# Sliding-window attention and a routed feed-forward, mixed by a gate: values projected transposed and turned on the core, and where the program jumps

## The chip, the core and the metric

The kernel runs on one core of a Trainium2 chip. The core has five engines with instruction streams of their own: TensorE (PE in the profile, its weight loads PEld), VectorE (DVE), ScalarE (ACT), GpSimd (POOL) and SyncE (SP), which here only issues DMA transfers. They meet through semaphores. SBUF is the on-chip memory, PSUM the eight banks that TensorE writes, HBM the memory outside the core. The metric is the time on the device in microseconds (us), the median of several runs.

## The reference

2048 tokens of 512 numbers in bf16. One branch is attention with 32 heads of 16 and a causal window of 256, the other a feed-forward that only the eight tokens with the largest router value pass. A sigmoid gate mixes them.

```python
def _A_ref(x, wqkv, wo):                       # S = 2048, D = 512
    H = 32; Dh = 16; W = 256
    q, k, v = split(x @ wqkv)                  # each by heads
    scores = einsum("bhqd,bhkd->bhqk", q, k) * Dh ** -0.5
    mask = (i - j >= 0) & (i - j < W)
    p = softmax(where(mask, scores, -1e9))
    return merge_heads(einsum("bhqk,bhkd->bhqd", p, v)) @ wo

def _B_ref(x, w_r, w_gate, w_up, w_down):      # w_gate, w_up: 512 x 1792
    r = x @ w_r
    idx = argsort(-r)[:, :8]                   # the top 8 tokens
    y = (silu(x[idx] @ w_gate) * (x[idx] @ w_up)) @ w_down
    return x.at[idx].add(y * sigmoid(r[idx]))

g = sigmoid((x * gate_w).sum(-1))              # x = A_x; _B_ref gets B_x in the call
out = g * _A_ref(x, wqkv, wo) + (1 - g) * _B_ref(x, ...)
```

The kernel reads A_x for both branches.

## The kernel before, in words

There are two programs in it. `fast_path` takes the softmax without subtracting a maximum; it adds up a flag that says whether all sums stayed in range. `general_path` is a slow one for other inputs; it does not run here. At the end every engine loads the flag and branches: to `fk_done`, or to `fk_general`.

**Chunks and units.** The 32 heads are done in 4 chunks c of 8 heads (128 columns). A chunk has 64 units, one for each block of 32 keys, so there are 256 units u. A unit (`s_unit`) is two score matmuls on TensorE (L690: the blocked keys Kbd against 288 queries QT, one for each half of the heads), one exponential on ScalarE (L697: 128 partitions x 576 columns from PSUM to P in SBUF) and, for each two units, one multiply by the mask on GpSimd (L704). P lies in a ring `PT` of RING slots, two slots a unit. `pv` (L725) multiplies P with the values: for each block of 128 queries, 34 columns of `Vbd` at a time (heads of 16 columns, and a column of ones that sums P); VectorE then takes the reciprocal of the sums (L740) and multiplies (L744), and a transposing DMA (`tr_dma`, L772) puts the result into OT, from which the output is projected (`wo_pair`, L788) and mixed (`out_evict`, L778).

**Projections.** x is brought in transposed, as XT, by transposing DMAs (L474) in pieces of 2, 2, 4, 4 and 4 tiles of 128 tokens. Q and K of a chunk are projected in squares of 512 tokens (`qk_pair`; 16 matmuls, L583); VectorE casts both to SBUF (L561, L564) and spreads K into Kbd with four masked multiplies (L569). The first square goes in two halves through `qk_first` (L604, L612, L615). Two PSUM bank pairs serve all work but the scores, and pass from one item to the next.

**Values.** `v_pair` (two chunks) and `v_two` (two chunks at once) project V with the tokens on the partitions (L626, L648). VectorE casts into `Vn` (L637, L660), and each piece is written to a scratch in HBM, `vsc` (L639, L663). `v_read` (L672) reads it back, for each group of 32 partitions, in another order of tokens, since `Vbd` needs each block of 32 keys on the 32 partitions of a head group, and zeros in the places of the other head. The zeros are written once at the start, by ScalarE (L530) and four DMAs (L534).

**Router.** `wrg_item` (L813) transposes the two weight rows of router and gate, `z_item` (L826) projects all tokens on them, `top_item` turns r into a row by way of a DMA (`f_r_row<-f_rT`) and searches the top 8 (L854, L855); ScalarE takes the sigmoid of these (L856). Then come a gather of eight rows, the feed-forward (`gu_item`, `silu_item`, `down_item`), a scatter into a copy of x, and `reload_x`, which loads that copy for the mix.

**What sets the order.** Operations are logged with a key (about the unit where they belong) and with costs and latencies; `schedule` walks through them, gives each engine what is ready with the smallest key, and so writes one fixed row of instructions for each engine, which then run in that order. A table `SHIFT` adds an offset to the keys of named groups. Each engine stops at an instruction whose semaphore isn't up yet.

**Blocks of code.** The engines' rows stand in one block; it ends with a barrier, then `values_load` and the branch:

```python
        bad = nc.values_load(flag[0:1, 0:1])                           # L1054
        ...
            br = eng.br_cond(bad < 1, "fk_done", "fk_general")         # L1058
            if et == mybir.EngineType.PE:
                br.branch_hint(S.hint["pe"])
            if et == mybir.EngineType.SP:
                br.branch_hint(S.hint["sp"])
        with nc.body("fk_general"):
            ...
            general_path(nc, *args)
            nc.br("fk_done")
        nc.switch_bb("fk_done")
```

The code of `general_path` lies between the branch and `fk_done`. A hint (a prefetch of the branch's target) stands 40 operations ahead of the end on TensorE and 8 on SyncE.

## Time and profile before

| | us |
|---|---|
| median of 3 runs | 203.36 (202.37 to 203.96) |
| the profiled execution | 203.8 |
| its span, first to last instruction | 202.1 |
| TensorE / ScalarE / VectorE / GpSimd busy | 168.3 / 147.3 / 110.7 / 87.6 |
| the 256 exponentials (L697) | 140.9 |
| casts of V (L637, L660) | 5.2 and 5.7 |

Times in the profile count from the first instruction. Busy time says how long an engine had something to do, not that it set the pace; the idle time before a group of instructions and what ended it (the arrow) say who waited for whom. "PEclk" is the clock granted to TensorE, 1.00 being full. An instruction is named by engine, line (L), operation and output<-input, with the number of instructions behind an x.

### The profile page before, as it was taken

What the parts mean: (1) busy time and instruction counts of PE and PEld (TensorE: products, weight loads), DVE (VectorE), ACT (ScalarE), POOL (GpSimd) and SP (SyncE); (2) the same over time, 40 slices, a digit from 0 to 9 for tenths busy, and PEclk for the clock granted to TensorE, in tenths of its full rate; (3) what the DMA queues carried; (4) which work ended last, traced back from release to release, by engine and by line L of the source; (5) the groups of instructions that cost most, each with busy time, mean ns of one, the idle gap of its engine ahead of it and who ended that gap; (6) DMA issues with size and microseconds to landing.
All of it is one profiled execution on the core that took longest, in us unless ns stands there. A gap on an engine that the chain in (4) does not pass through costs nothing.

```text
span 202.1 us, 10131 instructions
## 1 busy us (share of the span) xinstructions
PE 168.3 (83%) x4568; PEld 108.3 (54%) x4568; DVE 110.7 (55%) x287; ACT 147.3 (73%) x266; POOL 87.6 (43%) x142
## 2 busy tenths in 40 slices
PE   7639898899887699869977989999793889999970
PEld 2435656568465455636845536665562456476430
DVE  5503709837353935833625564499974354454780
ACT  6733860999992969657977897996897699999200
POOL 4112420555562355433543555663554345566200
PEclk9975759999996669856999999999999589999998
DMA  7997143168665733562175671378253102032221
GB/s 147 221 200 172 51 110 98 42 157 170 152 174 174 220 74 73 150 190 58 39 218 144 165 136 30 81 182 213 57 135 113 29 1 82 20 118 68 80 84 63
DMA packets 45217, 23.71 MB, mean 117 GB/s; under 512 B 32352, under 2 KB 44912, under 8 KB 45040
## 3 DMA queue, kind: packets, MB, share of 16 engines
q1 hardware_dynamic: 44048, 22.73, 45.4%
q8 instruction: 37, 0.61, 1.3%
q10 hardware_dynamic: 1056, 0.26, 0.6%
q14 instruction: 12, 0.10, 0.2%
q0 software_dynamic: 64, 0.02, 0.0%
HBM read 14.03 MB, written 6.43 MB: 101 GB/s over the span
## 4 chain that ended last, share of the span: by engine, by line
PE 42%; ACT 26%; DVE 13%; SPq 6%; DMA 5%; issue 5%; POOL 0%; DVEq 0%
ACT f_PT L697 26%; PE f_ps L583 12%; PE f_ps L690 11%; PE f_ps L725 8%; SPq L474 5%; PE f_ps L648 3%; PE f_ps L626 3%; PE f_ps L788 2%; DMA f_xw<-f_xc 2%; DVE f_Kr L564 2%; DVE f_QT L561 2%; DMA f_r_row<-f_rT 2%; DVE f_Kbd L569 2%; DVE f_xw L935 2%; PE f_ps L919 2%
## 5 line engine op out<-in xcount | busy, mean ns | idle before, releaser
L697 ACT ACTIVATE f_PT<-f_ps 128x576 bf16<-128x576 f32 (+7 forms) x256 | 140.9, 623 | 35.6 <-PE f_ps L690 23.4
L704 POOL TENSOR_TENSOR f_PT<-f_PT,f_MK 128x256 bf16<-128x256 bf16 (+1 forms) x128 | 83.4, 652 | 99.4 <-ACT f_PT L697 98.9
L690 PE MATMUL f_ps<-f_QT,f_Kbd 64*128 64x288 bf16 (+7 forms) x512 | 76.8, 300 | 9.7 <-ACT f_PT L697 7.5
L725 PE MATMUL f_ps<-f_Vbd,f_PT 64*128 64x34 bf16 x2880 | 56.7, 177 | 10.7 <-issue 5.0
L725 PEld LDWEIGHTS f_ps<-f_Vbd,f_PT 64*128 64x128 bf16 x2880 | 52.3, 95 | 22.6 <-issue 9.9
L690 PEld LDWEIGHTS f_ps<-f_QT,f_Kbd 64*128 64x128 bf16 x512 | 25.6, 97 | 35.3 <-ACT f_PT L697 28.9
L583 PE MATMUL f_ps<-f_XT,f_W 64*128 64x512 bf16 x240 | 43.8, 441 | 0.5 <-DVE f_On L744 0.5
L569 DVE TENSOR_SCALAR f_Kbd<-f_Kr,f_hm 128x512 bf16<-128x512 bf16 (+1 forms) x64 | 23.5, 426 | 0.1
L564 DVE CAST f_Kr<-f_ps 128x512 bf16<-128x512 f32 x15 | 10.2, 683 | 18.9 <-PE f_ps L583 18.8
L583 PEld LDWEIGHTS f_ps<-f_XT,f_W 64*128 64x128 bf16 x240 | 12.5, 107 | 8.8 <-issue 2.5
L561 DVE CAST f_QT<-f_ps 128x512 bf16<-128x512 f32 x15 | 10.2, 683 | 12.7 <-PE f_ps L583 12.7
L788 PE MATMUL f_ps<-f_wo,f_OT 64*128 64x512 bf16 x112 | 16.6, 377 | 0.1
L740 DVE RECIPROCAL f_RC<-f_ps 128x16 f32<-128x16 f32 (+1 forms) x33 | 8.2, 247 | 14.9 <-PE f_ps L725 13.7
L778 DVE SCALAR_TENSOR_TENSOR f_outt<-f_ps,f_g_f,f_xw 128x512 bf16<-128x512 f32 x16 | 11.4, 746 | 8.3 <-PE f_ps L788 8.2
L626 PE MATMUL f_ps<-f_W,f_XT 64*128 64x128 bf16 x256 | 13.9, 252 | 1.2 <-DMA f_XT<-in_A_x_dram 1.1
L744 DVE TENSOR_TENSOR f_On<-f_ps,f_RC 128x256 bf16<-128x256 f32 (+1 forms) x33 | 13.6, 412 | 0.7
L626 PEld LDWEIGHTS f_ps<-f_W,f_XT 64*128 64x128 bf16 x256 | 11.0, 112 | 3.5 <-issue 1.8
L648 PE MATMUL f_ps<-f_W,f_XT 64*128 64x256 bf16 x128 | 9.9, 270 | 0.2
L935 DVE TENSOR_SCALAR f_xw<-f_xw,f_omg_f 128x512 bf16<-128x512 bf16 x16 | 7.4, 500 | 2.8 <-DMA f_xw<-f_xc 2.8
L660 DVE CAST f_Vn<-f_ps 128x256 bf16<-128x256 f32 x16 | 5.7, 417 | 4.9 <-PE f_ps L648 4.9
L648 PEld LDWEIGHTS f_ps<-f_W,f_XT 64*128 64x128 bf16 x128 | 5.9, 94 | 1.8 <-PE f_ps L648 0.5
L637 DVE CAST f_Vn<-f_ps 128x512 bf16<-128x512 f32 x8 | 5.2, 672 | 2.8 <-PE f_ps L626 2.8
(91 smaller groups left out, 74.5 us busy)
## 6 DMA issues: line engine op xcount, KB each, us to landing
f_xc<-in_A_x_dram SPq DMA_DIRECT2D x8, 256.0 KB, 4.2
f_xw<-f_xc SPq DMA_DIRECT2D x8, 256.0 KB, 3.7
out_dram<-f_outt SPq DMA_DIRECT2D x16, 128.0 KB, 1.7
f_xw<-in_B_w_gate_dram SPq DMA_DIRECT2D x8, 224.0 KB, 3.2
f_xw<-in_B_w_up_dram SPq DMA_DIRECT2D x8, 224.0 KB, 3.5
f_xw<-in_B_w_down_dram SPq DMA_DIRECT2D x7, 256.0 KB, 4.1
f_vsc<-f_Vn SPq DMA_DIRECT2D x8, 136.0 KB, 3.2
f_Vbd<-f_vsc SPq DMA_DIRECT2D x16, 68.0 KB, 2.5
```

Of the source, the lines that this page charges most:

```text
L561: dve(lambda e: e.tensor_copy(out=dst, in_=bank(b)), r=[T(b)], w=[("QT", c % 2, tc)], cost=610, key=key, rel=rel)
L564: dve(lambda e: e.tensor_copy(out=Kr[:, tc, :], in_=bank(b)), r=[T(b)], w=[("Kr", tc)], cost=610, key=key, rel=rel)
L569: dve(lambda e, h=h, k0=k0, q=q: e.tensor_scalar(out=Kbd[:, c % 2, k0:k0 + w8, h, :], in0=Kr[:, tc, 32 * w8 * q:32 * w8 * q + 32 * w8].rea ...
L583: return e.matmul(bank((A, B)[which])[:, w0:w1], W[R, kc, f0:f0 + 128], XT[R, kc, 512 * tc + w0:512 * tc + w1], start=st, stop=False, skip ...
L626: return e.matmul(bank((A, B)[b])[:, 128 * i:128 * i + 128], XT[R, kc, 128 * a:128 * a + 128], W[R, kc, f0:f0 + 128], start=st, stop=False ...
L648: return e.matmul(bank((A, B)[b])[:, 256 * i:256 * i + 256], XT[R, kc, 128 * a:128 * a + 128], W[R, kc, f0:f0 + 256], start=st, stop=False ...
L690: ins = e.matmul(bank(b0 + s)[:, 0:n], Kbd[R, c % 2, kb, :, :].rearrange("p h k -> p (h k)"), QT[R, c % 2, 32 * kb:32 * kb + n], start=Tru ...
L697: act(lambda e: e.activation(out=dst, in_=ps[:, b0:b0 + 2, 0:n], func=ACT.Exp, scale=0.25), r=[T(b0), T(b0 + 1)], w=[("P", slot // 2), ("E ...
L704: pool(lambda e: e.tensor_tensor(out=v, in0=v, in1=m, op=ALU.mult), r=[("P", sl // 2), ("P", sl // 2 + 1)] + MKR, w=[("Pm", sl // 4)], cos ...
L725: ins = e.matmul(bank((A, B)[rg])[:, col:col + 34], PT[R, o0:o0 + 128], Vbd[R, c % 2, :, kb % 4, kb // 16, s, (kb // 4) % 4, :], start=(kb ...
L744: dve(lambda e: e.tensor_tensor(out=dst, in0=both(h_)[:, :, 0:68 * nj].rearrange("p b (j g d) -> p b j g d", d=17, g=4)[:, :, :, :, 0:16], ...
L788: return e.matmul(bank((A, B)[o])[:, w0:w1], OT[R, c, 128 * a:128 * a + 128], wo[R, c, w0:w1], start=st, stop=False, skip_group_check=True ...
```

## The change

1. **Values.** `v_order` (GpSimd) reorders the columns of W for V into `WV`. `v_pair`, now for all chunks, projects V transposed: WV is the stationary side and 512 tokens move, so that the features lie on the partitions. VectorE transposes each bank in squares of 32 into `TV` (f32), and two masked multiplies write it into `Vbd`, one for each of the two heads, which also writes the zeros. `Vn`, `vsc`, `v_two`, `v_read` and the zeros at the start are gone; the column of ones is written by two VectorE operations in `late_consts`, behind the first K.
2. **Jumps.** There is no barrier block. A few first operations of ACT, DVE, POOL and SP ("early": the first loads, the table, some constants) and all of TensorE's stand in the first block; each engine then jumps over the general code to `fk_main`. There the rest stands, each engine waits for the flag's semaphore, loads the flag and branches to `fk_done`, which now lies right behind. Hints: at the start on ACT and SP, 60 operations ahead of its jump on PE.
3. **Router** keys move by 2 to 4 units (22 to 26, 24 to 28, 40 to 42); RING goes from 40 to 48; costs and latencies in the list change, and 91 lines of `SHIFT` with them.

The core of the diff:

```diff
-RING = 40
+RING = 48
@@ emit
+            for i, op in enumerate(self.ops[e][:n]):
+                if e == "pe" and i == n - HINT_AT:
+                    hint = h.mark_branch_hint_location()
+                self.one(e, h, op)
+            br = h.br("fk_main")
+            if hint is not None:
+                br.branch_hint(hint)
...
+    def main(self):
+        for e in self.ENGS:
+            h = self.handle[e]
+            for op in self.ops[e][self.n_early[e]:]:
+                self.one(e, h, op)
+            h.wait_ge(*self.flag)
@@ fast_path
+        for op in S.log:
+            op.early = True
...
+        def late_consts():
+            dve(lambda e: e.memset(pads, 0.0), r=[("Krb", 0)], w=["pads"], cost=1900, key=K0 + 150)
+            for b in range(2):
+                dve(lambda e, b=b: e.tensor_scalar(out=Vbd[:].rearrange("p c s k b d -> p (c s k) b d")[:, :, b, 16], in0=bass.AP(ones_c, 0, [[128, 128], [0, 2], [1, 128]]),
+                                                   scalar1=pm[:, b:b + 1], scalar2=None, op0=ALU.mult), ...)
@@ v_pair
-                return e.matmul(bank((A, B)[b])[:, 128 * i:128 * i + 128], XT[R, kc, 128 * a:128 * a + 128], W[R, kc, f0:f0 + 128],
+                return e.matmul(bank((A, B)[b]), WV[R, c % 2, kc, :], XT[R, kc, t0:t0 + 512],
                                 start=st, stop=False, skip_group_check=True, tile_position=(R.start, 0))
...
-                dve(lambda e, b=b, g=g: e.tensor_copy(out=Vn[:, g, c % 2, :, :, :, 0:16], in_=bank((A, B)[b]).rearrange("p (i s h d) -> p h s i d", i=4, s=2, h=4)), ...)
-                dma(lambda e, g=g: e.dma_start(vsc[c].rearrange("h p g x -> p h g x")[:, :, g, :], Vn[:, g, c % 2].rearrange("p h s b d -> p h (s b d)")), ...)
+                dve(lambda e, b=b: e.transpose(out=TV[:, b, :], in_=bank((A, B)[b])), r=[T((A, B)[b])], w=[("TV", b)], cost=720, key=key, rel=h_)
+                for q in range(2):
+                    dst = Vbd[:, c % 2, :, 16 * tc:16 * tc + 16, q, 0:16].rearrange("p s k d -> p k s d")
+                    (dve if VM[q] == "dve" else pool)(
+                        lambda e, b=b, q=q, dst=dst: e.tensor_scalar(out=dst, in0=TV[:, b, :].rearrange("p (k s d) -> p k s d", s=2, d=16),
+                                                                     scalar1=pm[:, q:q + 1], scalar2=None, op0=ALU.mult), ...)
@@ router
-        at(21, lambda: wrg_item(22))
-        at(21.1, lambda: z_item(24))
-        at(36, lambda: top_item(40))
+        at(25, lambda: wrg_item(26))
+        at(25.1, lambda: z_item(28))
+        at(38, lambda: top_item(42))
@@ the r row's transfer, as the list counts it
-            dma(lambda e: e.dma_start(r_row[0:1, :], rT[:, :]), r=["rT"], w=["r_row"], key=key)
+            dma(lambda e: e.dma_start(r_row[0:1, :], rT[:, :]), r=["rT"], w=["r_row"], key=key, lat=4000)
@@ end
+        nc.switch_bb("fk_main", parent=first)
+        S.main()
+        bad = nc.values_load(flag[0:1, 0:1])
+        nc.br_cond(bad < 1, "fk_done", "fk_general")
+        nc.switch_bb("fk_done", parent=first)
```

What the list makes of it is seen in three places. First TensorE's row at the start, before: L604 is the first K and Q, L690 scores (four instructions are two units), L626 values, L813 the router's transpose. L583, K and Q of the next square, follows further down, and the first L725 stands behind 22 units.

```order
L604 MATMUL f_ps<-f_XT,f_W 128x256 x16
L690 MATMUL f_ps<-f_QT,f_Kbd 128x288 x4
L626 MATMUL f_ps<-f_W,f_XT 128x128 x8
L690 MATMUL f_ps<-f_QT,f_Kbd 128x288 x2
L626 MATMUL f_ps<-f_W,f_XT 128x128 x12
L690 MATMUL f_ps<-f_QT,f_Kbd 128x288 x2
L626 MATMUL f_ps<-f_W,f_XT 128x128 x12
L813 MATMUL f_ps<-f_ident,f_wrow 128x8
```

The row at the same place in the changed kernel, where L614 is the first K and Q, L679 scores, L593 K and Q of the next square and L644 values:

```order
L614 MATMUL f_ps<-f_XT,f_W 128x256 x16
L679 MATMUL f_ps<-f_QT,f_Kbd 128x288 x8
L593 MATMUL f_ps<-f_XT,f_W 128x512 x4
L679 MATMUL f_ps<-f_QT,f_Kbd 128x288 x2
L593 MATMUL f_ps<-f_XT,f_W 128x512 x4
L679 MATMUL f_ps<-f_QT,f_Kbd 128x288 x2
L644 MATMUL f_ps<-f_XT,f_WV 128x512 x2
L593 MATMUL f_ps<-f_XT,f_W 128x512 x2
```

Four units instead of two come first, and the second square of K and Q goes ahead of the values. The router's transpose (now L802) has moved from behind 4 units of scores to behind 20, its projection (now L815) from behind 8 to 15 units to behind 27 to 30, the first PV (now L714) to behind 14, and the transpose of r from behind 54 units to behind 49. In ScalarE's row the sigmoid of the top 8 moves from behind 68 exponentials to behind 71.

Second, VectorE's row between the first K and the second half of V. Before (L637 V, L561 and L564 casts of Q and K, L569 Kbd, L830 and L833 the router's z):

```order
L615 TENSOR_SCALAR f_Kbd<-f_Kr,f_hm 128x8x32 x4
L814 COPY f_wrg<-f_ps 128x8
L637 CAST f_Vn<-f_ps 128x32x16 x2
L561 CAST f_QT<-f_ps 128x512
L564 CAST f_Kr<-f_ps 128x512
L569 TENSOR_SCALAR f_Kbd<-f_Kr,f_hm 128x8x32 x8
L830 COPY f_zr<-f_ps 128x32
```

After (L544 and L546 the constants, L574 and L571 casts of K and Q, L579 Kbd, L655 the transpose and L659 the multiplies of V):

```order
L625 TENSOR_SCALAR f_Kbd<-f_Kr,f_hm 128x8x32 x4
L544 MEMSET f_PT 128x49x48
L546 TENSOR_SCALAR f_Vbd<-f_ones_c,f_pm 128x256 x2
L574 CAST f_Kr<-f_ps 128x512
L571 CAST f_QT<-f_ps 128x512
L579 TENSOR_SCALAR f_Kbd<-f_Kr,f_hm 128x8x32 x4
L655 STREAM_TRANSPOSE f_TV<-f_ps 128x512 x2
L659 TENSOR_SCALAR f_Vbd<-f_TV,f_pm 128x16x2x16 x4
L571 CAST f_QT<-f_ps 128x512
```

The memset of P's gaps has moved from the program's start to behind the first K, and two casts have become two transposes and four multiplies.

Third, the end on VectorE, before (the last mixes, the flag, the end of the block with its barrier, the load of the flag, the branch) and after:

```order
L778 SCALAR_TENSOR_TENSOR f_outt<-f_ps,f_g_f,f_xw 128x512 [waits fd_15]
L1041 TENSOR_SCALAR flag<-f_ps 1x1 [waits fk_pe]
L266 UNCONDITIONAL_BRANCH
L1054 TENSOR_LOAD flag [waits barrier_Pool_Activation_PE_DVE_SP_release]
L1058 COMPARE_AND_BRANCH
```

```order
L767 SCALAR_TENSOR_TENSOR f_outt<-f_ps,f_g_f,f_xw 128x512 [waits fd_9]
L767 SCALAR_TENSOR_TENSOR f_outt<-f_ps,f_g_f,f_xw 128x512 [waits fd_11,fk_pe]
L1019 TENSOR_SCALAR flag<-f_ps 1x1 [waits fk_pe]
L1038 TENSOR_LOAD flag [waits fk_dve]
L1039 COMPARE_AND_BRANCH
```

The flag is loaded behind its own semaphore instead of a barrier. TensorE's row ends, after the last matmul, with its jump to `fk_main`.

## The prediction

> **What bounds the kernel now.** I read the page first (busy line, clock row), then busy time by stage, then the waits of ScalarE (ACT), then the stretches with the longest waits in order of time.

> ```profile
> span 202.1 us, 10131 instructions
> PE 168.3 (83%) x4568; PEld 108.3 (54%) x4568; DVE 110.7 (55%) x287; ACT 147.3 (73%) x266; POOL 87.6 (43%) x142
> PEclk9975759999996669856999999999999589999998
> ```

> No engine is full on average. The clock row is the hint: slices (5 us each) with 5 or 6 come after stalls. So I cut the span where it changes.

> ```profile
> core 0: us, PE busy (x) PEld busy (x) DVE busy (x) ACT busy (x) POOL busy (x), PEclk, DMA share, GB/s
> 8.00:36.00 28.00, 22.04 (x489) 14.60 (x489) 11.35 (x38) 13.06 (x23) 6.77 (x10) 0.76 0.58 131
> 36.00:62.00 26.00, 23.04 (x780) 16.46 (x780) 13.89 (x32) 24.76 (x48) 14.77 (x23) 0.97 0.59 134
> 62.00:75.00 13.00, 10.03 (x181) 6.24 (x176) 7.86 (x17) 7.37 (x14) 5.09 (x7) 0.67 0.65 179
> 197.30:202.10 4.80, 0.00 (x0) 0.00 (x0) 0.00 (x0) 0.00 (x0) 0.00 (x0) 0.81 0.18 58
> ```

> In 36 to 62 ACT is full (24.8 of 26 us): there the exponentials set the pace. In 8 to 36 it works 13 of 28 us, in 62 to 75 7.4 of 13, and in the last 4.8 us nothing works. The losses lie in these places, and its waits say so:

> ```profile
> ACT f_PT L697 <- PE f_ps L690: 23.4, 33, 3.3
> ACT f_PT L697 <- PE f_ps L725: 10.7, 6, 5.2
> ACT f_sg L856 <- DVE f_top L854: 3.9, 1, 3.9
> ```

> The opening in order of time, exponentials first (count behind the x), then four of TensorE (PE): its last wait for x, the router's transpose, the first PV and a piece of K/Q at full clock:

> ```profile
> 8.03 1.19 ACT L697 ACTIVATE f_PT<-f_ps 128x576 bf16<-128x576 f32 x2 [0.39 <-PE f_ps L690]
> ...
> 14.30 0.65 ACT L697 ACTIVATE f_PT<-f_ps 128x576 bf16<-128x576 f32 x1 [3.18 <-PE f_ps L690]
> ...
> 21.06 4.84 ACT L697 ACTIVATE f_PT<-f_ps 128x576 bf16<-128x576 f32 x8 [3.26 <-PE f_ps L690]
> ...
> 35.36 1.19 ACT L697 ACTIVATE f_PT<-f_ps 128x576 bf16<-128x576 f32 x2 [5.19 <-PE f_ps L725]
> ```

> ```profile
> 9.37 0.40 PE L626 MATMUL f_ps<-f_W,f_XT 64*128 64x128 bf16 x8 [1.11 <-DMA f_XT<-in_A_x_dram]
> ...
> 13.74 0.16 PE L813 MATMUL f_ps<-f_ident,f_wrow 8*128 8x8 bf16 x1 [3.06 <-DMA f_wrow<-in_gate_w_dram]
> ...
> 32.00 1.63 PE L725 MATMUL f_ps<-f_Vbd,f_PT 64*128 64x34 bf16 x116 [0.65 <-DVE f_g_f L836]
> ...
> 34.19 1.04 PE L583 MATMUL f_ps<-f_XT,f_W 64*128 64x512 bf16 x8
> ```

> Three waits, 3.2 + 3.3 + 5.2 = 11.7 us. The first: PE stands 3.06 us at the router's tiny transpose (L813) until its weights land. The second follows at half clock. The third: the ring of P holds 20 units, 20 exponentials are done at 30.1, and the 21st waits until 35.36 for the first PV, which stands behind 22 units in PE's row and begins at 32.0.

> **The change part by part.** (1) Opening. The router's transpose now stands behind 20 units of scores instead of 4 and its projection behind 27 to 30, the first PV behind 14 instead of 22, the ring holds 24 units. Nothing in PE's row waits for those router weights any more. What is late next is the second K/Q square: its x is there at 9.4 (the L626 row, on the same tiles); its 16 matmuls take 2.1 us by the L583 row (eight in 1.04, a pair 0.26), and four score pairs between them 0.6 (288 of 512 columns, 0.15 each): 12.1; two casts of 0.68 (L564 below), so unit 8 has its Q at 13.5, against 8.03 + 8 x 0.605 (the row of eight: 4.84/8) = 12.9 at ACT's own pace. Unit 20 then is at 8.03 + 20 x 0.605 + 0.6 = 20.7; I take 22, one more for what I don't see. Gain to there 35.36 - 22 = **13.4**.

> Whether VectorE (DVE) lets that happen:

> ```profile
> L564 DVE CAST f_Kr<-f_ps 128x512 bf16<-128x512 f32 x15 | 10.2, 683 | 18.9 <-PE f_ps L583 18.8
> L637 DVE CAST f_Vn<-f_ps 128x512 bf16<-128x512 f32 x8 | 5.2, 672 | 2.8 <-PE f_ps L626 2.8
> L660 DVE CAST f_Vn<-f_ps 128x256 bf16<-128x256 f32 x16 | 5.7, 417 | 4.9 <-PE f_ps L648 4.9
> L523 DVE MEMSET f_PT<- 128x1968 uint32 x1 | 1.7, 1698 | 1.3 <-PEq L1937 1.3
> ```

> ```profile
> 7.94 0.87 DVE L615 TENSOR_SCALAR f_Kbd<-f_Kr,f_hm 128x256 bf16<-128x256 bf16 x4
> ...
> 34.12 1.13 DVE L569 TENSOR_SCALAR f_Kbd<-f_Kr,f_hm 128x512 bf16<-128x512 bf16 x4
> ...
> 37.83 1.96 DVE L569 TENSOR_SCALAR f_Kbd<-f_Kr,f_hm 128x512 bf16<-128x512 bf16 x4
> ```

> No row shows the transpose in squares of 32. It reads 512 f32 columns of PSUM as L637 does: 0.67 each, with 0.28 (an SBUF pass of 512) and 1.34 (twice the cast) as ends. The masking multiply reads 512 f32 from SBUF: between 0.28 (L569 at 34.12, 1.13 for four, GpSimd (POOL) idle) and 0.67; I take 0.45, near the 0.49 of the x4 at 37.83. A V pair is 2 x 0.67 + 4 x 0.45 = **3.2 us** (1.7 to 5.4), eight pairs 25 against the 10.9 of L637 and L660: 14 more (3 to 32). In the opening DVE's row is, from 8.8 (end of the first Kbd): memset 2.0 (1698 x 49/41 gaps of the ring), ones 0.6, two casts from 12.1 to 13.5, four half Kbd 0.9 (the L615 row), V pair 3.2: 17.6. PV behind 14 units is wanted at 8.03 + 14 x 0.605 + 0.6 = 17.1. So it fits, barely.

> ```profile
> 36.63 0.67 POOL L704 TENSOR_TENSOR f_PT<-f_PT,f_MK 128x256 bf16<-128x256 bf16 x1 [5.82 <-ACT f_PT L697]
> 37.77 0.67 POOL L704 TENSOR_TENSOR f_PT<-f_PT,f_MK 128x256 bf16<-128x256 bf16 x1 [0.47 <-ACT f_PT L697]
> ```

> POOL stood still for 5.8 us ahead of 36.6, so beside the first L569 row no mask ran, and beside the second one did: same shape, 0.28 against 0.49. [...]

> (2) Work put off. By unit 20 the kernel before had projected V of the second half and z; now they come between units 22 and 34, with the last K/Q square.

> ```profile
> L826 PE MATMUL f_ps<-f_wrg,f_XT 64*128 64x2 bf16 x128 | 2.8, 163 | 0.0
> ```

> Twelve units leave PE 12 x (0.605 - 0.15) = 5.5 us beside the scores. It needs V 2.1 and K/Q 2.1 (16 matmuls each, as above), z 2.8, PV 1.1 (80 by the 32.00 row): 8.1, so 2.6 over; DVE I put at 2 over, as V's 3.2 and the square's 3.1 (two casts, four Kbd of 0.44) meet there. I charge **+4.5** (1 to 8).

> (3) Router chain.

> ```profile
> 63.73 2.28 DVE L854 MAX8 f_top<-f_r_row 1x8 f32<-1x2048 bf16 x1 [4.76 <-DMA f_r_row<-f_rT]
> 66.05 0.21 ACT L856 ACTIVATE f_sg<-f_top 1x8 f32<-1x8 f32 x1 [3.92 <-DVE f_top L854]
> ```

> ACT stands 3.9 us at the sigmoid, behind 68 units. In its new row it stands behind 71, and the transpose of r goes from behind 54 to behind 49: 22 units instead of 14 between the two, some 5 us more. The wait should go (0 to -3.9): **-3**, and -1 for the half clock behind it (0.67 in 62 to 75). The two searches of 2.3 us stay on DVE.

> (4) The rest. Units 68 to 255 see five V pairs of 3.2 instead of 8 us of casts: 8 us more DVE work in a stretch where ACT is often the pace. No row excludes all or nothing: **+2** (-2 to +8). The 48 transfers of the V scratch and four of zeros leave the SP queue; ACT waits for none of them by the rows above, so 0.

> (5) The two ends.

> ```profile
> 195.44 0.39 PE L1038 MATMUL f_ps<-f_ones_f,f_okc 128*1 128x1 f32 x10
> 196.88 0.13 DVE L1041 TENSOR_SCALAR flag<-f_ps 1x1 int32<-1x1 f32 x1
> 196.33 0.99 SPq L780 DMA_DIRECT2D out_dram<-f_outt  x2
> L1058 SPq COMPARE_BRANCH  x1: 78/78/78, 198.3 to 198.3; - x1
> out_dram<-f_outt SPq DMA_DIRECT2D x16, 128.0 KB, 1.7
> ```

> The branch runs at 198.3, the span ends at 202.1: a jump taken costs 3.7 us, though SP has a prefetch hint ahead of it. After the change the last branch falls through, but the last output (issued 197.0, median 1.7 to land) holds the end to about 199.0, and PE has a jump of its own behind its last matmul: 195.8 + 3.7 + 0.6 for flag and branch = 200.1 if its hint fails. Gain 2.0 to 3.1: **-2.5**. The early jumps: DVE's memset is done at about 0.9, the jump makes it 4.6, 13 small operations of about 0.1 (four L509 in 0.34) make 5.9; ACT is ready to jump at 3.3 (below), so 7.0.

> ```profile
> 3.10 0.20 ACT L526 ACTIVATE f_okc<-f_ones_f 1x1 f32<-1x1 f32 x1
> ...
> 3.21 0.34 DVE L509 TENSOR_SCALAR f_hm<-f_hf 128x1 f32<-128x1 f32 x4
> ...
> 6.17 0.42 DVE L612 CAST f_Kr<-f_ps 128x256 bf16<-128x256 f32 x1 [2.32 <-PE f_ps L604]
> 7.02 0.61 ACT L609 CAST f_QT<-f_ps 128x256 bf16<-128x256 f32 x2
> ```

> In the kernel before DVE's first cast is at 6.2 and ACT's at 7.0. Both are just in time, so 0, hidden by the first x transfers; 0 to +2 if the fetch is slower among them. POOL's copies of W for V (eight pairs of small copies) run while it waits for ACT: 0.

> Sum: -13.4 + 4.5 - 4 + 2 - 2.5 = -13.4. The profiled execution took 203.8 (span 202.1 and 1.7 around it), 0.4 above the median of 203.36: 203.8 - 13.4 = 190.4, and **190** as a median.

> **The rivals.** A: VectorE sets the opening. If V of the first half is ready at 22 instead of 17.6 (memset, ones, a square and V in one row, multiplies at 0.67) units 22 to 24 stand some 4 us at the ring's end, and the router's 3.9 may stay: 194 to 198. For it: DVE's row above has no slack; against: it is busy 11.35 of 28 us there now.
> B, slower: DVE sits in ACT's path in every chunk. Each V pair stands ahead of a K/Q cast in its row, and ACT needs that Q eight units later (4.8 us). If a chunk's cast comes within 3.2 us of its need, a whole pair goes on the path. From about 1.7 us for each of eight pairs (13.4/8) the gain is gone; with all of 3.2 to 4.0 (25.6 to 32, less 10.9) and only the first and third wait and the tail won (3.2 + 5.2 + 2.5), 203.8 + 14.7 - 10.9 = 207.6, up to 214. Against: DVE is busy 13.9 of 26 us where ACT is full, and K/Q of a chunk is queued some 24 units ahead.
> C: another wait takes the place of L813: the later x transfers keep PE idle, the clock halves anyway, and only the tail is won: 201 to 203. Against: PE's list has no wait for x behind 9.4.
> D: the last branch still fetches: 190 + 2.5 = 192.5.

> **How the numbers follow.** Forecast (184 to 196) 0.60, A 0.22, D 0.05, C 0.05, B 0.08. Low end 181: all bounds on the good side (-13.4 + 1 - 4.9 - 2 - 3.1 = -22.4). High end 199 takes in A and leaves out C and B. Within 1% (2 us, about what this kernel's runs can tell) lies C: 0.05; slower 0.08; faster 0.87.

> **What would show it.** Right: no ACT wait over 1.5 us before unit 20, the 21st exponential at 20 to 24 us, clock 1.00 there; transposes near 0.67 and multiplies near 0.45; no wait at the sigmoid; nothing over 3 us between flag and end. Wrong: ACT waits for PV at units 22 to 26 with DVE full (A), Q casts behind V pairs as the releaser of scores in chunks 1 to 3 (B), PE waiting for x after 10 us (C).

## Result: 179.6 us, and the profile after

The changed kernel took 179.57 us (median of 4 runs, 177.81 to 180.76) against 203.66 for the kernel before beside it: a ratio of 0.879 (0.870 to 0.889). The forecast was 190, with a range of 181 to 199; the time lies below it. The profiled execution took 180.07 us (span 178.7). Runs of one kernel scatter by 2 to 9 us, the longer ones mostly at a lower granted clock; ratios leave out those over 1.5% above their kernel's fastest, and of such runs are the profile of the kernel before (its fastest run on record took 197.3 us) and six below: the reach of 20, the late jumps, the shortened multiplies, the early weights, the edited opening, the old path with a ring of 48.

The page of the changed kernel, first its span, the busy times and the clock by slices of 4.5 us:

```profile
span 178.7 us, 9562 instructions
PE 153.7 (86%) x4307; PEld 93.8 (52%) x4310; DVE 127.9 (72%) x316; ACT 140.2 (78%) x263; POOL 93.1 (52%) x148
PEclk9999999999999879999999999999999999999998
```

VectorE has 17 us more to do and the kernel is 23 us shorter. The clock row is the second thing to see: one dip is left, where before there were eight slices at 5 or 6. (The first slices say nothing: this trace's clock record begins at 10.04 us.)

Where it came from is seen by cutting both spans at the same units: from the first exponential to unit 20, to unit 64, to the end of unit 255, to the end. Before:

```profile
core 0: us, PE busy (x) PEld busy (x) DVE busy (x) ACT busy (x) POOL busy (x), PEclk, DMA share, GB/s
8.00:35.40 27.40, 21.44 (x485) 14.50 (x487) 10.84 (x36) 12.46 (x22) 6.77 (x10) 0.75 0.58 132
35.40:59.80 24.40, 21.70 (x720) 15.15 (x717) 14.39 (x33) 23.16 (x45) 13.75 (x22) 1.00 0.62 139
59.80:188.80 129.00, 111.81 (x3207) 72.30 (x3206) 75.11 (x183) 105.68 (x194) 64.69 (x99) 0.89 0.43 111
```

After:

```profile
10.20:24.20 14.00, 11.05 (x187) 5.01 (x185) 13.53 (x30) 11.39 (x20) 8.89 (x10) 1.00 0.58 129
24.20:50.50 26.30, 23.60 (x820) 15.94 (x822) 21.53 (x52) 23.20 (x46) 15.28 (x25) 1.00 0.45 122
50.50:166.80 116.30, 103.54 (x3072) 65.03 (x3073) 82.03 (x195) 103.38 (x194) 66.98 (x103) 0.99 0.37 94
166.80:178.70 11.90, 7.63 (x207) 4.31 (x207) 7.47 (x23) 0.00 (x0) 0.12 (x1) 0.94 0.28 92
```

The third rows are what the forecast missed: 129.0 us have become 116.3, with the same 194 activations (105.7 and 103.4 us busy) and 7 us more work on VectorE. ScalarE's waits before and after (its rows in the prediction: 23.4, 10.7 and 3.9 us):

```profile
ACT f_PT L686 <- PE f_ps L679: 13.9, 18, 2.1
ACT f_QT L619 <- PE f_ps L614: 5.3, 2, 4.8
ACT f_PT L686 <- PE f_ps L714: 4.0, 3, 1.8
```

The waits on PV (now L714) fell from 10.7 to 4.0 us, the one at the sigmoid is gone. Behind unit 72 alone, where the forecast missed most, ScalarE's waits were, before and then after:

```profile
ACT f_PT L697 <- PE f_ps L690: 12.5, 19, 1.8
ACT f_PT L697 <- PE f_ps L725: 5.5, 5, 1.9
```

```profile
ACT f_PT L686 <- PE f_ps L679: 9.0, 11, 1.9
ACT f_PT L686 <- PE f_ps L714: 2.8, 2, 1.8
```

The opening in order of time:

```profile
3.90 0.15 DVE L523 TENSOR_SCALAR f_hi_t<-f_hi_t 128x1 int32<-128x1 int32 x1 [2.90 <-issue]
...
6.33 3.57 PE L614 MATMUL f_ps<-f_XT,f_W 128*128 128x256 bf16 x16 [1.24 <-DMA f_XT<-in_A_x_dram]
...
10.26 4.45 ACT L686 ACTIVATE f_PT<-f_ps 128x576 bf16<-128x576 f32 x8 [0.80 <-PE f_ps L679]
...
13.65 1.66 DVE L546 TENSOR_SCALAR f_Vbd<-f_ones_c,f_pm 128x256 bf16<-128x256 bf16 x2
...
16.81 0.65 ACT L686 ACTIVATE f_PT<-f_ps 128x576 bf16<-128x576 f32 x1 [2.10 <-PE f_ps L679]
```

The first exponential comes at 10.26, 2.2 us later than before (8.03), since the first K and Q begin at 6.33 instead of 5.38 and take 3.57 us, where the same 16 matmuls took 2.06 before and 1.91 in experiment 1. Unit 8 waits 2.10 us for its Q, behind the column of ones (1.66 us for two instructions, expected 0.6). Still unit 20 is at 24.2 instead of 35.4. The transposes and multiplies of V:

```profile
L659 DVE TENSOR_SCALAR f_Vbd<-f_TV,f_pm 128x512 bf16<-128x512 f32 x32 | 18.7, 626 | 0.0
L655 DVE STREAM_TRANSPOSE f_TV<-f_ps 128x512 f32<-128x512 f32 x16 | 10.5, 693 | 3.7 <-PE f_ps L644 3.7
```

### The profile page after: what moved, and what is told of

Same layout as the page of the kernel before. It is cut to its first block, busy times and chain, and to the rows that moved or that the text cites. A ratio compares the mean times of both kernels' runs of the same rounds, so it can differ in the third digit from the quotient of the medians.

```text
span 178.7 us, 9562 instructions
## 1 busy us (share of the span) xinstructions
PE 153.7 (86%) x4307; PEld 93.8 (52%) x4310; DVE 127.9 (72%) x316; ACT 140.2 (78%) x263; POOL 93.1 (52%) x148
## 4 chain that ended last, share of the span: by engine, by line
PE 46%; DVE 22%; ACT 19%; DMA 6%; issue 5%; POOL 1%; SPq 0%
ACT f_PT L686 19%; PE f_ps L679 11%; PE f_ps L714 11%; PE f_ps L593 7%; PE f_ps L644 7%; PE f_ps L777 5%; DVE f_Vbd L659 4%; DMA f_idxT<-f_idxu 3%; DMA f_XT<-in_A_x_dram 3%; DVE f_Kbd L579 2%; DVE f_QT L571 2%; PE f_ps L614 2%; PE f_ps L908 2%; DVE f_Kr L574 2%; DVE f_outt L767 2%
## 5 line engine op out<-in xcount | busy, mean ns | idle before, releaser
L686 ACT ACTIVATE f_PT<-f_ps 128x576 bf16<-128x576 f32 (+7 forms) x256 | 137.8, 627 | 19.0 <-PE f_ps L679 13.9
L693 POOL TENSOR_TENSOR f_PT<-f_PT,f_MK 128x256 bf16<-128x256 bf16 (+1 forms) x128 | 87.1, 683 | 63.5 <-ACT f_PT L686 62.7
L679 PE MATMUL f_ps<-f_QT,f_Kbd 64*128 64x288 bf16 (+7 forms) x512 | 72.3, 280 | 8.3 <-ACT f_PT L686 6.4
L714 PE MATMUL f_ps<-f_Vbd,f_PT 64*128 64x34 bf16 x2880 | 54.8, 174 | 8.4 <-issue 3.7
L714 PEld LDWEIGHTS f_ps<-f_Vbd,f_PT 64*128 64x128 bf16 x2880 | 50.4, 93 | 19.1 <-issue 5.5
L679 PEld LDWEIGHTS f_ps<-f_QT,f_Kbd 64*128 64x128 bf16 x512 | 24.7, 93 | 42.5 <-ACT f_PT L686 36.9
L593 PE MATMUL f_ps<-f_XT,f_W 64*128 64x512 bf16 x240 | 36.5, 377 | 0.3 <-DVE f_On L733 0.3
L579 DVE TENSOR_SCALAR f_Kbd<-f_Kr,f_hm 128x512 bf16<-128x512 bf16 (+1 forms) x64 | 23.6, 418 | 0.1
L644 PE MATMUL f_ps<-f_XT,f_WV 64*128 64x512 bf16 x128 | 20.1, 382 | 0.1
L659 DVE TENSOR_SCALAR f_Vbd<-f_TV,f_pm 128x512 bf16<-128x512 f32 x32 | 18.7, 626 | 0.0
L733 DVE TENSOR_TENSOR f_On<-f_ps,f_RC 128x256 bf16<-128x256 f32 (+1 forms) x33 | 13.5, 409 | 0.5
L655 DVE STREAM_TRANSPOSE f_TV<-f_ps 128x512 f32<-128x512 f32 x16 | 10.5, 693 | 3.7 <-PE f_ps L644 3.7
L593 PEld LDWEIGHTS f_ps<-f_XT,f_W 64*128 64x128 bf16 x240 | 11.2, 94 | 3.4 <-DVE f_On L733 0.6
L574 DVE CAST f_Kr<-f_ps 128x512 bf16<-128x512 f32 x15 | 10.4, 693 | 3.3 <-PE f_ps L593 3.2
L571 DVE CAST f_QT<-f_ps 128x512 bf16<-128x512 f32 x15 | 10.2, 681 | 3.0 <-PE f_ps L593 2.9
L644 PEld LDWEIGHTS f_ps<-f_XT,f_WV 64*128 64x128 bf16 x128 | 6.0, 96 | 2.7 <-PE f_ps L644 1.1
L777 PEld LDWEIGHTS f_ps<-f_wo,f_OT 64*128 64x128 bf16 x112 | 5.3, 94 | 2.8 <-PE f_ps L749 0.5
L635 POOL COPY f_WV<-f_W 128x256 bf16<-128x256 bf16 x8 | 3.1, 412 | 3.5 <-DMA f_W<-in_A_wqkv_dram 3.5
## 6 DMA issues: line engine op xcount, KB each, us to landing
out_dram<-f_outt SPq DMA_DIRECT2D x16, 128.0 KB, 2.0
f_W<-in_A_wqkv_dram SPq DMA_DIRECT2D x4, 128.0 KB, 3.5
```

The source lines that it names most:

```text
L571: dve(lambda e: e.tensor_copy(out=dst, in_=bank(b)), r=[T(b)], w=[("QT", c % 2, tc)], cost=610, key=key, rel=rel)
L574: dve(lambda e: e.tensor_copy(out=Kr[:, tc, :], in_=bank(b)), r=[T(b)], w=[("Kr", tc)], cost=610, key=key, rel=rel)
L579: dve(lambda e, h=h, k0=k0, q=q: e.tensor_scalar(out=Kbd[:, c % 2, k0:k0 + w8, h, :], in0=Kr[:, tc, 32 * w8 * q:32 * w8 * q + 32 * w8].rea ...
L593: return e.matmul(bank((A, B)[which])[:, w0:w1], W[R, kc, f0:f0 + 128], XT[R, kc, 512 * tc + w0:512 * tc + w1], start=st, stop=False, skip ...
L644: return e.matmul(bank((A, B)[b]), WV[R, c % 2, kc, :], XT[R, kc, t0:t0 + 512], start=st, stop=False, skip_group_check=True, tile_position ...
L659: lambda e, b=b, q=q, dst=dst: e.tensor_scalar(out=dst, in0=TV[:, b, :].rearrange("p (k s d) -> p k s d", s=2, d=16), scalar1=pm[:, q:q + ...
```

## Experiments

The diffs are shortened; "..." and words in the place of code mark what is left out.

**1. The jumps.** The changed kernel, same rows, with the blocks in their old places:

```diff
-            br = h.br("fk_main")            # no early part; fast path, then general_path
+        bad = nc.values_load(flag[0:1, 0:1]); br_cond(bad < 1, "fk_done", "fk_general")
```

> The changed kernel, same rows on each engine, with the blocks as before: nothing is early, no engine jumps at the start, the fast path stands ahead of the general one, and the last branch is taken over the general code (hints 40 and 8 operations ahead, as before; no barrier). Theory: the early jumps cost nothing that is seen and the end saves 3: 182 to 184. Rival: the first exponential of the changed kernel was 2.2 us late because of the early jumps: then it comes at 8 us, and what is lost at the end is won at the start, 179 to 181.5.

It took 180.9 us (178.1 to 182.0), which cannot be told from the changed kernel and lies where the rival had it. Its opening and its flag:

```profile
5.42 1.91 PE L608 MATMUL f_ps<-f_XT,f_W 128*128 128x256 bf16 x16 [0.33 <-DMA f_XT<-in_A_x_dram]
...
7.86 1.74 ACT L680 ACTIVATE f_PT<-f_ps 128x576 bf16<-128x576 f32 x3 [0.57 <-PE f_ps L673]
...
174.03 0.13 DVE L1013 TENSOR_SCALAR flag<-f_ps 1x1 int32<-1x1 f32 x1
```

Without the jumps x lands 0.9 us earlier (5.42 against 6.33), and K and Q take 1.91 us (16 x 256 columns at 0.21 us for 512, the pace of experiment 8's bench at full clock, would be 1.7): the first exponential is at 7.86. The late x is not this one execution's: the first K and Q begin at 6.2 to 7.7 us in all ten profiles with early jumps, and at 5.2 to 5.7 in the ten without. That the fetch of the jumps' code delays x is the author's guess; no run shows it. From the flag to the end of the program it takes 180.6 - 174.0 = 6.6 us, in the changed kernel 180.07 - 176.85 = 3.2 and before 203.8 - 196.9 = 6.9. So the end saves 3.4 to 3.7 us, and the start loses up to 2.4 of them; between the two the runs show no difference that can be told.

**2. The opening inside the same rows.** Two edits: three more warming matmuls and half of the memset moved ahead of the first K; and, in another kernel, VectorE's and GpSimd's constants ahead of their jumps.

```diff
-            pe(lambda e: e.matmul(bank(2), ones_c[:], ...))                 # 9 times
+            pe(lambda e, i=i: [e.matmul(...) for _ in range(4 if i == WARM - 1 else 1)][-1])
-            dve(lambda e: e.memset(pads, 0.0), r=[("Krb", 0)], ...)
+        dve(lambda e: e.memset(pads0, 0.0), ..., cost=0, key=K0 + 7)         # 25 of 49 gaps
```

> The changed kernel, rows as they are: 12 warming matmuls instead of 9, and half of the memset of P's gaps ahead of the first K on VectorE (the other half in its place). Theory: first exponential at 8.7 to 9.5 instead of 10.3, unit 8 at 14.5 to 15.5 instead of 16.8, and since the rows stay, no long wait later: 177 to 178.5. Rival (the starting phase of the clock decides the first 2 us in each run, and later waits take the rest): 179 to 180.5.

```diff
+        for e, k in (('dve', 14), ('pool', 6)):
+            for op in self.ops[e][:k]:
+                op.early = True
```

> The changed kernel, rows as they are; VectorE's 14 small constants and GpSimd's identity stay ahead of their jumps, so that these engines jump at about 2.4 and 1.6 us instead of 0.9. If the code fetched at the jumps delays the first x transposes (0.9 us late against the blocks in the old places): the delay stays, as the fetch only moves: first exponential at 9.5 to 10.5, 179 to 181. If only the constants' lateness mattered: no change either, since VectorE waited 2.2 us for K. If the jump now ends behind K (after 5.4 us): slower by up to 1.

The first took 178.12 us (176.83 to 180.68), ratio 0.885 (0.877 to 0.893), the second 181.7 (179.73 to 183.56), 0.902 (0.892 to 0.911).

```profile
6.32 1.91 PE L619 MATMUL f_ps<-f_XT,f_W 128*128 128x256 bf16 x16 [0.43 <-DMA f_XT<-in_A_x_dram]
...
8.77 2.28 ACT L691 ACTIVATE f_PT<-f_ps 128x576 bf16<-128x576 f32 x4 [0.57 <-PE f_ps L684]
...
14.89 1.73 ACT L691 ACTIVATE f_PT<-f_ps 128x576 bf16<-128x576 f32 x3 [1.25 <-PE f_ps L684]
```

With more warming K and Q take 1.91 instead of 3.57 us, though x lands as late as in the changed kernel; unit 8 is 1.9 us earlier, and unit 255 still 2.4 (163.8 against 166.2). The ratio cannot be told from the changed kernel's, and that the warming did it is not shown. The late jumps have nine warming matmuls and x as late, and K and Q take 1.91 there too:

```profile
6.17 1.91 PE L618 MATMUL f_ps<-f_XT,f_W 128*128 128x256 bf16 x16 [1.43 <-DMA f_XT<-in_A_x_dram]
```

In the eight profiles with early jumps and nine warming matmuls these 16 matmuls take from 1.91 to 3.57 us, in the two with twelve 1.91 and 2.40. So the rival, that the starting phase of the clock's windows decides, is not refuted, and not shown either: in the changed kernel the clock's record begins at 10.04, behind these matmuls. The first exponential of the late jumps is at 8.90, earlier than the 9.5 to 10.5 expected, and the time brought nothing.

**3. The router's stand in the kernel before.** All its rows as they are, only the weights' loads are issued earlier:

```diff
-        SP: ... dma_start(wrow[0:4, :], ...), dma_start(wrow[4:8, :], ...)   # behind the x transposes
+        ACT: the same two, behind its two W loads
```

> The kernel before, all rows as they are but for one thing: the two loads of the router's weights are issued by ScalarE's queue behind its two W loads (at about 2 us) instead of behind SyncE's x transposes, so that the router's transpose finds its data. Theory (the stand of 3.06 us and the half clock behind it made unit 8 late): unit 8 at 15 to 18 instead of 21.1, projection of z done earlier, first PV and 21st exponential 3 to 6 us earlier, time 196 to 200. Rival (PV and the ring take what is won there): 21st exponential within 1.5 us of 35.4, time 201 to 204.

It took 200.01 us (195.96 to 201.0) against 203.68 (199.59 to 208.19); the two scatters touch, so what counts here is the order of events. L823 is the router's transpose here, L707 the exponentials, L735 PV:

```profile
11.03 0.17 PE L823 MATMUL f_ps<-f_ident,f_wrow 8*128 8x8 bf16 x1
...
15.89 4.76 ACT L707 ACTIVATE f_PT<-f_ps 128x576 bf16<-128x576 f32 x8 [2.14 <-PE f_ps L700]
...
32.35 1.19 ACT L707 ACTIVATE f_PT<-f_ps 128x576 bf16<-128x576 f32 x2 [8.38 <-PE f_ps L735]
```

The stand at the transpose is gone and unit 8 comes 5.2 us earlier. Then the wait for the first PV grows from 5.19 to 8.38 us, and 3.0 us are left at the 21st exponential. The stand alone was worth some 3 us; the rest of the opening's gain was held by the first PV, behind 22 units. Which of the earlier PV and the longer ring frees it was not tried alone.

**4. Parts alone, and lists computed anew.** Three kernels put one part into the kernel before, two edited the changed one; in all five the list was computed again with a table made for other rows.

```diff
 before: wrow loads  lat=3000 -> lat=20000                       # router later
 before: v_pair, v_two, v_read -> v_order, v_pair, late_consts    # new values, router at 4 units
 the same, without "wrg_item/22/pe": -205, with "pv/14/pe": -255.5 # new values, router at 25 units
 after:  RING = 48 -> 52
 after:  WARM = 9 -> 12, ones on ScalarE, half memset early, each with its cost
```

> The kernel before, with one number changed in its list: the two router weight rows count as landing after 20 us, so that the router's transpose stands behind 24 units of scores instead of 4 and its projection behind 25 to 34; values still go through HBM, jumps and ring as before. Theory O (the order of the opening pays, and the router's stand is most of it): no 3 us wait of TensorE at the transpose, full clock from there, 25th exponential at 28 to 31 us (before 37.6, changed kernel 26.4), time 194 to 200. Rival V (the values' path pays, since the scratch in HBM holds the first PV and the second square back): 25th exponential not before 34, time 201 to 205.

> The kernel before with the new values path alone (projected transposed, turned by VectorE, no scratch); the router's transpose still stands behind 4 units, ring 40, block and end as before (one line of the table, an early PV's, is taken out so that a row comes about). Theory O: TensorE still stands about 3 us at the router's transpose and the clock halves, 25th exponential at 33 to 37, time 199 to 205. Rival V: 25th exponential at 27 to 30, time 190 to 195. In both, the VectorE multiplies stay off the path (no wait of the exponentials on a values pair in the chunks 1 to 3).

> The kernel before with the new values path and the router's transpose behind 25 units (its line of the table taken out); ring 40, block, barrier and end as before. Theory O and rival V both expect the opening of the changed kernel: 25th exponential at 25 to 28, time 184 to 190 (the end is worth 1.4 to 3.4 of what is left to 179.6). A third theory, that the changed kernel's jumps, ring of 48 and new table are needed for the rest, expects 190 to 196: the opening is won, but the stretches at half clock behind the router's and the feed-forward's work stay.

> The changed kernel with a ring of 52 (26 units) instead of 48. If the ring is still what the exponentials meet: 176 to 178.5, PV waits (4.0 us in three) gone. If 24 units are enough: 178.5 to 181.

> The changed kernel with three edits in its opening: 12 instead of 9 warming matmuls, so that TensorE is busy until x lands; half of the memset of P's gaps ahead of the first K instead of behind it; the column of ones by ScalarE, which idles there, instead of VectorE beside the masks. Theory (first exponential late by half clock at the first K and Q, 1.5 us, and unit 8 late by ones and memset, 2.1 us): first exponential at 8.5 to 9.3 instead of 10.3, no wait over 1 us at unit 8, 176 to 178.5. Rival (the clock's windows fall where they fall, and what is won at unit 8 is lost at the next wait): 178.5 to 181.

| | us | ratio to before |
|---|---|---|
| router later | 216.19 (214.7 to 220.0) | 1.075 (1.042 to 1.108) |
| new values, router early | 214.46 (212.6 to 215.3) | 1.070 (1.045 to 1.094) |
| new values, router later | 203.80 (203.4 to 205.3) | 1.019 (0.999 to 1.039) |
| ring 52 | 202.41 (201.1 to 205.5) | 1.017 (0.986 to 1.047) |
| edited opening | 199.88 (195.6 to 204.1) | 0.992 (0.978 to 1.005) |

All five missed what was expected. New values with the router later do have the opening (25th exponential at 26.8 us, changed kernel 26.4), and lose it all afterwards: units 64 to 255 take 133.3 us. The edited opening won 1.8 us to unit 24 and then lost 16.66 in one wait; ring 52 has such a wait of 13.40:

```profile
84.78 1.74 ACT L690 ACTIVATE f_PT<-f_ps 128x576 bf16<-128x576 f32 x3 [16.66 <-PE f_ps L718]
```

There the new list has put projections of the next chunk ahead of the PV that frees the ring's slots (in the edited opening 52 matmuls of 512 columns between 67.0 and 83 us, and no scores). These times say nothing on the parts; they say that the rows are worth some 20 us, and that a part is to be judged without the table or with the rows held.

**5. Without the table.** SHIFT emptied in both kernels, with a ring of 40 and of 48.

```diff
-SHIFT = { "v_order/-32/pool": -50.5, ... }
+SHIFT = { }
```

> The kernel before with its table SHIFT empty: the list sets the rows by keys and costs alone. Theory P (the new path and the router's place bring the gain of units 64 to 255 whatever the table): the table is worth the same to both kernels, some 5 to 12 us here: 207 to 215, with 64 to 255 at 130 to 140 us (128.4 with its table). Rival S (the new table brings it): also 207 to 215; the two are told apart by the next run.

> The changed kernel with its table SHIFT empty. Theory P: 64 to 255 stays at 116 to 122 us, time 183 to 190, some 20 below the kernel before without its table. Rival S: 64 to 255 goes back to 128 to 140 us and the time to 195 to 210; what is left to the kernel before without its table is the opening and the end, 5 to 12 us.

> The changed kernel with its table empty and the ring at 40 instead of 48. If the ring matters (a late PV stops the exponentials 20 instead of 24 units later): 2 to 6 us slower than the one with 48 and the table empty, with more waits of the exponentials on PV. If not: within 2 us of it.

> The kernel before with its table empty and a ring of 48 instead of 40: fourth corner of a square (old or new path with its jumps, ring 40 or 48, no table); the others took 209.05 (old, 40), 195.77 (new, 40) and 191.41 (new, 48). If ring and path add up: 204 to 206. If the ring pays whatever path there is, and more where PV comes late behind the scratch: 198 to 203. If the ring pays only with the new path: 207 to 210.

| us, ratio to before; units 64 to 255 in the profile | ring 40 | ring 48 |
|---|---|---|
| kernel before | 209.05, 1.035 (1.027 to 1.042); 129.0 | 208.95, 1.050 (1.032 to 1.069); 133.1 |
| changed kernel | 195.77, 0.964 (0.957 to 0.971); 129.2 | 191.41, 0.952 (0.944 to 0.960); 120.8 |

Without tables the change is worth 17.6 us; 13.3 of them come at a ring of 40 (9.5 us in the profiles ahead of unit 64), and 4.4 from the longer ring, which gives the old path nothing. In units 64 to 255 the change without its ring gains nothing (129.0 and 129.2); with the ring of 48 the stretch falls by 8.4, into the range of theory P, though the time is just above its 190; with the table it falls by another 5.1 (to 115.7). ScalarE's waits on PV go the same way, first ring 40, then 48:

```profile
ACT f_PT L686 <- PE f_ps L714: 12.9, 6, 3.7
```

```profile
ACT f_PT L686 <- PE f_ps L714: 4.4, 4, 2.1
```

Each corner is one list, so a few us may be its luck; the next run is free of that.

**6. The ring with the rows held.** Ring of 48, all rows as in the changed kernel, and a wait more for the exponentials, as a ring of 40 would have it:

```diff
+        for u in range(20, 256):      # where the rows allow it
+            self.expo[u].sync.append(last PV that reads unit u - 20)
```

> The changed kernel, rows and ring of 48 as they are, but the exponential of unit u waits for the PV of unit u - 20, as it would with a ring of 40, in 209 of 236 places; in the other 27 (units 20, 21, 28 to 31, 68, 92, 100, 101, 116 to 119, 124, 125, 132 to 134, 148 to 151, 252 to 255) the PV stands behind the scores of u + 2 in TensorE's row, so that the rows would lock and no wait is added. If the longer ring pays by its slack all along: 182 to 188 with waits of the exponentials on PV up from 4 us. If it pays only by the rows that it allows (those 27 places): 178.5 to 181.

189.53 us (187.32 to 192.9), ratio 0.940 (0.930 to 0.950): 10.0 us slower than the changed kernel. The waits on PV (L749 here), 4.0 us in three in the changed kernel, are now:

```profile
ACT f_PT L721 <- PE f_ps L749: 17.7, 15, 2.4
```

Units 64 to 255 take 124.5 us, 8.8 more. So these rows use the reach of 24 units all along. In 27 places the rows could not even run with 20, so the longer ring also allows the order itself. Rows laid out for 20 might lose less, so the 10.0 says what the reach is worth in these rows. Part of it is the clock, which stands at 0.95 in that stretch instead of 0.99. The late jumps of experiment 2, the same rows without the added waits, give a measure: their profile has as much half clock in units 72 to 255 (13.7 us; the changed kernel 3.4) and takes 116.0 us there, the changed kernel 111.3, the reach of 20 119.2. By that some 3 us are the waits alone, and the rest goes with the clock.

**7. VectorE's work with the rows held.**

```diff
+                    if c: dve(... tensor_scalar(out=scr[:, b, q], in0=TV[:, b, :], ...), cost=0)   # doubled
```

> The changed kernel, rows of all engines as they are; in the chunks 1 to 3 every masked multiply of the values is done a second time into a scratch tile, behind the first: 24 more instructions of 0.63 us, 15 us more for VectorE (127.9 to 143). Theory (VectorE's work for the values lies off the path, which the prediction charged with 2 us, up to 8): 179 to 182. Rival (it is on the path, and the gain of units 64 to 255 is net of it): 186 to 195, with waits of the exponentials behind Q casts in the chunks 1 to 3.

```diff
-dst, TV[:, b, :] ... 16 blocks of keys
+dst[:, 0:1], ... [:, 0:1]        # chunks 2 and 3: 1 block of 16
```

> The changed kernel, rows as they are; in the chunks 2 and 3 each of the 16 masked multiplies writes 1 of its 16 blocks of keys (15 of 16 blocks keep the values of the chunks 0 and 1, so that part of the result is left out): some 16 x 0.53 = 8.5 us less for VectorE. Counterpart of the doubled multiplies, which cost 18 us for 15. If VectorE's work for the values is on the path in these rows: units 128 to 255 take 66 to 71 instead of 72.9 us, time 173 to 177. If the rows have hidden it and only work that they do not reckon with costs: 72 to 73.5 us, time 178.5 to 180.5.

```profile
L664 DVE TENSOR_SCALAR f_scr<-f_TV,f_pm 128x512 bf16<-128x512 f32 x24 | 15.3, 638 | 0.0
```

```profile
L659 DVE TENSOR_SCALAR f_Vbd<-f_TV,f_pm 128x512 bf16<-128x512 f32 x16 | 9.9, 668 | 0.0
L659 DVE TENSOR_SCALAR f_Vbd<-f_TV,f_pm 128x32 bf16<-128x32 f32 x16 | 3.5, 258 | 0.0
```

15.3 us more took the kernel to 197.79 us (194.6 to 202.47), 0.976 (0.967 to 0.984): the theory "off the path" fell, and the cost is above the rival's 186 to 195. It is 18.2 us in the medians and 15.5 between the profiled executions, 13.0 of these in units 64 to 255 (128.7), where the clock is 0.92. The weight loads of PV wait 7.0 us for casts of K there, in the changed kernel 0.4, so what comes late is casts of K rather than of Q. Masks held up on GpSimd are not the cause: they take 0.694 us in the mean against 0.683. Some 6 us less (16 x 0.37, not the 8.5 expected) gave 180.69 (176.1 to 182.18), 0.883 (0.867 to 0.899): nothing that can be told. Units 128 to 255 took 71.3 instead of 72.9 us, between the two ranges, and other kernels with these rows have 71.9 to 74.4. As far as the two show, the rows just hide what they were laid out for, and have no room for more.

**8. The clock.** First a filler of 400 columns ahead of each group of the feed-forward's matmuls of 8 columns in the kernel before, then the clock by itself, behind the changed kernel's flag.

```diff
+                    if wh == 0: e.matmul(bank(A)[:, 112:512], ones_c[:], <128 x 400>, start=True, stop=True)
```

> The kernel before; each of the 7 groups of feed-forward matmuls of 8 columns (the gate's, at 79 to 82 us) is led by one matmul of 128 rows x 400 columns into unused columns of the same bank, result unread: 2800 columns, 1.2 us of TensorE more. Theory (the clock halved at 84 to 94 because the 3.4 us before moved few columns through TensorE, though it was busy 73%): full clock from 81 to 95, units 88 to 104 take 11 instead of 14.9 us, time 2 to 5 us below the kernel before. Rival (few columns have nothing to do with it, the clock follows the idle time): the stretch stays at half clock, time 0 to 2 us above.

```diff
+        BENCH = ((40, 512), (300, 8), (60, 512), (300, 16), (60, 512), (300, 32), (60, 512))   # count, columns
```

> The changed kernel with its blocks in the old places, and behind its flag seven stretches of matmuls on TensorE (128 rows, results unread): 40 of 512 columns, 300 of 8, 60 of 512, 300 of 16, 60 of 512, 300 of 32, 60 of 512. It measures the clock alone; its time is not compared. Theory C (a window of 3.4 us in which few columns move halves the clock for the next one, however busy TensorE is): full clock at the end of each 512 stretch, half behind the stretches of 8 and of 16 columns, so that the next 512-column matmuls take 0.43 instead of 0.21 us at first; 32 columns open. Rival I (idle time halves it): TensorE is not idle in any stretch, so full clock from the first 512 stretch to the end.

The filler kept the clock at 1.00 from 77 to 95, where it had stood at 0.50 from 84.2 to 94.5; but another stretch (99 to 103) fell, and the time is 202.67 us (199.29 to 205.05), 0.999 (0.991 to 1.007), not the 2 to 5 us less of the theory. Units 88 to 104 take 12.9 us instead of 14.9 (11 expected): the stretch was cured, the kernel not.

```profile
87.80:95.00 7.20, 7.01 (x237) 5.29 (x233) 4.79 (x12) 6.96 (x13) 4.11 (x7) 1.00 0.53 89
```

The bench, in windows of 3.41 us (columns as above: the clock is the third number from the end):

```profile
180.95:184.37 3.42, 3.42 (x17) 1.54 (x16) 0.00 (x0) 0.00 (x0) 0.00 (x0) 1.00 0.00 0
184.37:187.78 3.41, 3.41 (x130) 3.29 (x129) 0.00 (x0) 0.00 (x0) 0.00 (x0) 1.00 0.02 5
187.78:191.19 3.41, 3.41 (x135) 3.41 (x132) 0.00 (x0) 0.00 (x0) 0.00 (x0) 0.50 0.02 5
...
208.26:211.67 3.41, 3.41 (x144) 3.41 (x140) 0.00 (x0) 0.00 (x0) 0.00 (x0) 1.00 0.02 5
211.67:215.09 3.42, 3.42 (x135) 3.42 (x132) 0.00 (x0) 0.00 (x0) 0.00 (x0) 0.50 0.02 5
...
232.15:235.57 3.42, 3.42 (x143) 3.42 (x140) 0.00 (x0) 0.00 (x0) 0.00 (x0) 1.00 0.02 5
235.57:238.98 3.41, 3.41 (x95) 2.70 (x92) 0.00 (x0) 0.00 (x0) 0.00 (x0) 1.00 0.02 5
```

By the records TensorE is busy all of every window (the ends of matmuls are modelled; weight loads fill the windows of 8, 16 and 32 columns alike). In a window of 512-column matmuls at full clock some 16 x 512 = 8192 columns pass (one matmul in 0.21 us; behind the stretch of 8 columns, at clock 0.50, their weight loads begin every 0.43 us from 192.76 on). By the matmuls that begin in them, the windows of 8 columns (128, and one of 512: 1,536) and of 16 columns (136 x 16 = 2,176, 0.27 of 8192) are followed by half clock, the window of 32 columns (136 x 32 = 4,352, 0.53) is not. So theory C came out and Rival I fell.

## Why the prediction was wrong, point by point

By its own steps, from the profiled executions (units by the start of their exponential):

| step | expected | measured |
|---|---|---|
| (1) start to unit 20 | -13.4 | -11.2 (35.4 to 24.2) |
| (2) work put off, units 20 to 64 | +4.5 | +1.9 (24.4 to 26.3) |
| (3) sigmoid and clock, units 64 to 72 | -4 | -4.3 (8.7 to 4.4) |
| (4) the rest, units 72 to 255 | **+2** (-2 to +8) | **-8.4** (119.7 to 111.3) |
| (5) the ends, behind unit 255's start | -2.5 | -1.4, and -0.3 outside the span |
| sum | -13.4 | -23.7 (203.8 to 180.07) |

**The step that failed is (4), "the rest".** It counted what VectorE gets there and nothing else. That cost did not show: the rows hide it, and taking 6 us of it away gains nothing that can be told (experiment 7). Two more profiles with the rows of before behind the opening, of experiments 3 and 8 (the latter with its filler), take 118.7 and 118.9 us there, so the 119.7 is not one execution's. What the step left out is the ring. Step (1) names the 24 units, but only for the opening; the row of waits on PV, 10.7 us in six, was quoted, and one of the six (5.19) was used. Waits of that kind run through the whole kernel: with the reach of 20 put back, units 72 to 255 take 119.2 us, and before they took 119.7. So in these rows 7.8 of the 8.4 hang on the ring; without tables it is 8.4 in units 64 to 255. There it pays only with the new path, which is why the two cannot be added up from before's profile alone: behind unit 72 before's own waits on PV are 5.5 us, of which 2.8 are left, and those on scores fall from 12.5 to 9.0. The same step also took no notice of the half clock behind unit 88 and at unit 200 (84.2 to 94.5 and 155.9 to 162.7, 17 us); in the changed kernel it is 3.4 us in that stretch (61.2 to 64.7). By the late jumps some 3 of the 7.8 are the wait itself and up to 4.7 the clock that goes with it; whether the waits bring on the half clock was not shown.

**Opening (1, 2).** The sum came out (-8.9 expected, -9.3 measured to unit 64), its parts less so. Unit 20 at 24.2 is just outside the 20 to 24 that were named. "Early jumps 0" was wrong: x lands 0.9 us later (later in every profile with them), and in this execution the first K and Q took 1.7 us longer than in experiment 1 (3.57 against 1.91), which the late jumps' execution did not; "0 to +2" held it, nearly. A wait over 1.5 us before unit 20 was to show the forecast wrong: there is one, 2.10 at unit 8. The router's stand (3.06) was worth 3.0 at the 21st exponential by itself, as priced.

**Sizes.** Transposes 0.693 (0.67 taken), multiplies 0.626 (0.45 taken, 0.67 as the upper end), so a V pair is 3.9 us, not 3.2. VectorE and GpSimd at work side by side took longer in the opening: a mask that began at 11.53, just ahead of the memset (11.71 to 13.73), took 3.19 us instead of 0.67, the next mask (14.68), beside the second instruction for the column of ones (13.94 to 15.31), 1.03, and the two instructions for that column 0.67 and 1.37. Over the whole kernel little of that is seen: the mean of the 128 masks went from 0.652 to 0.683 us. V's first half was ready at 21.3, near A's 22, and VectorE was busy 13.5 of the 14 us between the first exponential and unit 20, as A had it; yet the ring's end was not met, for PV begins on the first half of what it needs (20.17).

**The end (5).** From the flag on 3.4 to 3.7 us are saved instead of 2 to 3.1, 0.3 of them behind the last recorded instruction. But the last exponential to the flag takes 2.0 us longer (10.7 instead of 8.7), so 1.4 is left.

**The rivals.** B's mechanism is real, but for work that the rows don't reckon with: the doubled multiplies. C and D did not come: no wait of TensorE for x behind 10 us, and no fetch at the last branch (SyncE goes on 0.2 us behind it, before 3.7).

## What to carry to other kernels

A longer buffer ring is priced over the whole kernel, not where it was first seen to bind: add up all waits on the stage that frees its slots, and ask which of them the new reach takes away. That is a first price only (5.5 us here behind unit 72); what the reach is worth in the new rows (10.0) showed when it was taken away with the rows held. Where a list and a tuned table set the rows, a part that is put in or taken out alone throws the rows away (up to 20 us here): hold every engine's row and change one wait or one duration, or empty the table on both sides. An engine can be full without costing anything as long as the rows were laid out around its work; 15 us that they didn't know of cost 15.5 to 18.
